# Attention and a squared-ReLU feed-forward on one core: the small products of the attention joined into fewer runs, and a second buffer for the weight ring of the last block

## The chip, the core and the metric

The kernel runs on one core of a Trainium2 chip. Its engines each take their instructions in order: TensorE (PE in the profile; its weight loads are PEld), VectorE (DVE), ScalarE (ACT), GpSimd (POOL) and SyncE (SP), which here issues nearly all DMAs. The metric is device time in microseconds of one execution; lower is better.

## The reference

Per batch (8) and head (8), with 576 rows of 64 numbers: a softmax of q over the row, a softmax of k over the sequence, then two products. The result, 4608 rows of 512, goes through a feed-forward with a squared ReLU.

```python
q_s = exp(q - max(q, -1));  q_s = q_s / (sum(q_s, -1) + 1e-9)
k_s = exp(k - max(k, 2));   k_s = k_s / (sum(k_s, 2) + 1e-9)
kv = einsum('bhsd,bhse->bhde', k_s, v)
x  = einsum('bhsd,bhde->bhse', q_s, kv)      # -> x: 4608 x 512
h  = maximum(x @ w_in, 0)                    # w_in: 512 x 2048
out = (h * h) @ w_out                        # w_out: 2048 x 512
```

## The kernel before

Everything is float32. The products of the feed-forward split each operand in a high and a low part of type fp32r and add three products; in the profile each is a matmul on the full 128*128 array with 512 or 256 columns. The products of the attention (k^T v, called kv, and q kv, called x) have contractions or outputs of 64 and use parts of the array: kv runs in shape 128*64, x in shape 64*64, and as plain float32 each of their matmuls is two records in the trace.

The 4608 rows are eight tiles t of 512 rows (the first 512 rows of each batch) and one tile of the eight tails of 64 rows. While the feed-forward of tile t runs, the attention of batch t+1 is made between its matmuls. Stages, in order of time:

- Tile 0 (to about 132 us), with the attention of batches 0 and 1 and the conversion of the weights from raw words (ACT scales, DVE and POOL join and split them). Until the first data are there PE runs filler transposes (`idle`).
- Tiles 1 and 2 (to about 309 us): per slice f of the hidden dimension `h` (12 matmuls) and `acc` (12 matmuls).
- Tiles 3 to 6 (to about 665 us) by Strassen's scheme on blocks, with half-width products `h<-w,ring` and `h<-w,w`. Sums of weight blocks lie in DRAM (`w_sums`) and come through a ring of buffers.
- The joint block (to about 750 us): tile 7 and the tails together, eight steps n of seven products (`pair_p1` to `pair_p7`, 6 matmuls of 512 columns each), with the ring loaded anew in each step, and the results kept in DRAM (`keep`, `g_b<-c`).
- The last product (`out`, L2015), and the writing of the result.

Up to the joint block the program records its operations, and a planner (class `Planner`) orders them with estimated durations: `order` takes, of what could start next, what has the longest path behind it (`tail`), shifted by lists of random seeds (`SEEDS` for tile 0, `LATER` for the rest). `place` and `possible` pick and grant PSUM banks: the small products share two banks (`choices`), which the joining of weight words uses too. `due` and `mark` tie an operation to a point in the chain of full matmuls. The joint block and the last product are written in program order.

Small products, from batch 2 on: `kv_product` makes kv of two pairs of heads (p-1, p) into two banks, each pair one unit of the plan (10 matmuls of 65 columns; column 65 is the sum of k). `kv_of` scales them on ACT. `x_products` then makes x of both pairs into the same banks: in turn 0 the 64 tail columns and the first 320, in turn 1 the last 192; ACT and DVE copy them out after each turn. Each matmul of x is a unit of its own, so that the planner may place them apart.

The ring: `load_ring(n, first)` loads the blocks of step n, in four groups: `a11` (768 KB, with `a12` and `s2`), `s1` and `s3` (256 KB each) and `a22` (512 KB, with `s4`). For `a11` there are two buffers (n even, n odd). `s1`, `s3` and `a22` have one each, so the load of step n+1 is issued behind the product of step n that read it. SP issues loads and stores in program order, and waits where a store's data aren't ready yet.

Of the kernel before, what the change touches and what calls it, by code (L numbers as in the profile page):

```python
# [132 lines left out]
class Planner:  # L133
# [92 lines left out]

    def place(self, b):
# [58 lines left out]
    def order(self):  # L286
# [12 lines left out]
        while ready:  # L299
            able = []  # L300
            for n in ready:
                t = max(free.get(n.engine, 0.0), n.since)
                if self.locked and n.port:
                    t = max(t, port)
                if n.behind is not None:
                    if n.behind.start is None:
                        continue
                    t = max(t, n.behind.start + n.behind.busy)
                for b in n.buffers:
                    if b.placed is not None:  # L310
                        continue
                    at, _ = self.place(b)
# [62 lines left out]
def attention_ffn(  # L375
# [29 lines left out]
    P = 128  # L405
# [25 lines left out]
    LATER = (  # L431
# [5 lines left out]
    )  # L437
# [11 lines left out]
    DUE = 3  # L449
    BURST = 450  # L450
    ON_ACT = 0
# [509 lines left out]
    def kv_product(b, *pairs):  # L961
# [3 lines left out]
        n = D if b == 0 else D + 1  # L965
        for p, ps in zip(pairs, two):
            with plan.together():
                kr, vr = made.pop(("ek", b, p)), made.pop(("v", b, p))
# [9 lines left out]
                for k_part, c in parts:  # L978
                    for j in range(2):
                        rows = slice((j ^ turn) * D, (j ^ turn) * D + D)  # L980
                        cols = slice(j * (D + 1), j * (D + 1) + n)
                        if b == 0:
                            of = vr[:, j, c, :] if c < C else v_heads[tl, 2 * p + j, 0:D].only(p // 2)
                        else:
                            of = vr[:, c, cols] if c < C else v_tail[:, p * W + cols.start:p * W + cols.stop]
                        T.matmul(
                            out=ps[rows, 0:n], lhsT=k_part[:, j * D:(j + 1) * D], rhs=of,
                            start=(c == 0), stop=(c == C), n=2 * n + BURST * (c == j == 0 and b > 1),
                        )

    def kv_scale(b, *pairs):
# [9 lines left out]
    def kv_of(b, *pairs):  # L1001

        kv_product(b, *pairs)
        kv_scale(b, *pairs)
        for p, ps in zip(pairs, made["kvp", b]):
            kv = small([P, D], "kvs", f"kv_{b}_{p}")
            S.activation(out=kv, in_=ps[:, 0:D], func=AF.Copy, scale=made.pop(("ks", p)), n=100)
            made["kv", b, p] = kv

    def x_product(b, p, x):  # L1010
# [26 lines left out]
        if p == NP - 1:  # L1037
            Y.dma_start(out=x_tail[:, :, b * TL:(b + 1) * TL], in_=made.pop(("xt", b)), kb=128)

    def x_products(b, p, x, turn):  # L1040

        pair = p - 1, p
        kvs, qts = [made["kv", b, i] for i in pair], [made["qT", b, i] for i in pair]
        two = made["kvp", b]
        FIRST = M - SPLIT

        def burst(begin, end, at):

            for j in range(2):
                for i in range(2):  # L1050
# [3 lines left out]
                        rhs=qts[i][rows, begin:end], start=True, stop=True,  # L1054
                        n=end - begin - 16 + BURST * (i == j == 0),
                    )

        def out_of(begin, end, at):

            n = end - begin  # L1060
            for i, (eng, one) in enumerate(((S.copy, two[0]), (V.tensor_copy, two[1]))):
                touched = [(pair[i] // 2, h) for h in range(begin // HM, 2)]
                eng(
# [4 lines left out]
        if turn == 0:  # L1068
            burst(M, SQ, SPLIT - TL)
            burst(0, FIRST, SPLIT)  # L1070
            if p == 1:
                made["xt", b] = small([P, NP, TL], "xt", f"xt_{b}", 1)
            xt = made["xt", b]
            S.copy(out=xt[:, pair[0], :].only(pair[0]), in_=two[0][:, SPLIT - TL:SPLIT], n=TL)
            V.tensor_copy(out=xt[:, p, :].only(p), in_=two[1][:, SPLIT - TL:SPLIT], n=TL)
            if b == B - 1:
                to = slabs[X_RAW + p // 2].bitcast(F32)[:, :, b * TL:(b + 1) * TL]
                Y.dma_start(out=to, in_=xt[:, pair[0]:p + 1, :], kb=64)
            elif p == NP - 1:
                Y.dma_start(out=x_tail[:, :, b * TL:(b + 1) * TL], in_=xt, kb=128)  # L1080
            out_of(0, FIRST, SPLIT)
        else:
            burst(FIRST, M, 0)
            out_of(FIRST, M, 0)
            for key in ("kv", "qT"):
                for i in pair:
                    made.pop((key, b, i))
            made.pop(("kvp", b))

# [620 lines left out]
    def strassen_pair(t, n, x_next, acc):  # L1710

        if n % 2 == 0:
            made["AB"] = [ps_h.tile([P, M], F32, tag="h", name=f"h_{t}_{n}_{i}") for i in range(2)]
# [11 lines left out]

        def two_units(slot):
            plan.due = now + 2
# [4 lines left out]
            plan.due = now + 2  # L1732
            unit(1)
            plan.due = None
# [34 lines left out]
        S.activation(out=c1[:, HM:M].only(1), in_=c1[:, HM:M].only(1), func=AF.Relu, n=HM)  # L1769
        two_units(slot_b)  # L1770
        block_product(t, n, A, "a22", "t4", False)
# [4 lines left out]
        V.tensor_tensor(out=gl1, in0=c1, in1=gh1, op=ALU.subtract)  # L1776
        block_product(t, n, Bk, "s4", "b22", False)
        ring_load(t, n + 1, "a22")
        plus(c0[:, HM:M].only(1), u2)
# [309 lines left out]
    for n in range(PAIRS):  # L2089
        if n == 0:  # L2090
            split_x_of("t4")
            unit(3)
        z = pair_begin(n)
        pair_p1(z)
        if n + 1 < PAIRS:
            load_ring(n + 1, "a11")
        if n == PAIRS - 1:
# [7 lines left out]
        if old:  # L2105
            pair_p4(old)
            pair_p3(old)
            load_ring(n, "a22")
        if n == PAIRS - 1:
# [7 lines left out]
        pair_p5(z)  # L2117
        if n + 1 < PAIRS:
            load_ring(n + 1, "s1")
        else:  # L2120
            for i in range(4):
# [7 lines left out]
        pair_p7(z)  # L2129
        if n + 1 < PAIRS:  # L2130
            load_ring(n + 1, "s3")
        if n == PAIRS - 3:
# [107 lines left out]
```

## Time and profile before

| | |
|---|---|
| median of 3 runs | 832.23 us (832.22 to 834.82) |
| profiled execution, its own time | 832.21 us |
| its span in the trace | 830.4 us |
| PE busy | 807.0 us, 97% (5085 matmuls) |
| PEld, DVE, ACT, POOL busy | 83%, 71%, 59%, 15% |
| DMA moved | 180.59 MB, mean 217 GB/s |
| chain that ended last | PE 84%, DMA 9%, ACT 2%, SP's queue 2%, DVE 1% |

The profiled execution took the time of the median, so times of its trace can be set against the median directly; 1.8 us lie outside its span. The busy time of PE counts matmuls whose latency overlaps that of the next. So the distance from one matmul's start to the next one's is what tells the cost, not the mean duration of one.

### The profile page before, as it was taken

Reading aid. Unit: us, or ns where it says so; the run is one execution under the profiler, and the core shown is the slowest. Engines: PE = TensorE matmul, PEld = TensorE weight load, DVE = VectorE, ACT = ScalarE, POOL = GpSimd, SP = SyncE. Lnnn points to the kernel's source line nnn. Section 1 sums busy time; section 2 is a strip of 40 time slices with the busy share of each in tenths; the row PEclk is TensorE's granted clock in tenths of the full one; section 3 lists DMA queues with packets and bytes.
Section 4 is the critical chain, followed back from the end, with each engine's and each line's share of the span. In section 5 each row is a group of like instructions: output and inputs, shape, how many; then the busy total and the mean of one; then the engine's idle time right before and its main releaser. Section 6 shows DMA issues by size and latency. Waiting matters only on the chain.

```text
span 830.4 us, 14550 instructions
## 1 busy us (share of the span) xinstructions
PE 807.0 (97%) x5085; PEld 691.3 (83%) x5085; DVE 589.0 (71%) x1206; ACT 489.5 (59%) x943; POOL 126.4 (15%) x145
## 2 busy tenths in 40 slices
PE   7989999999999999999999999999999998889997
PEld 6678878888787889898998989898888887778886
DVE  6888977785687657777678777777776732237995
ACT  5888855454465456656666576566665645456452
POOL 4899881100000000000000000000000000000000
PEclk9999999999999999999999999999999999999999
DMA  9993126776435368977988878889977459989666
GB/s 273 387 344 106 39 55 178 238 216 194 110 97 150 93 156 257 270 218 203 271 265 236 262 238 260 236 240 258 273 227 216 135 196 329 319 289 375 194 194 100
DMA packets 217353, 180.59 MB, mean 217 GB/s; under 512 B 133184, under 2 KB 184896, under 8 KB 217280
## 3 DMA queue, kind: packets, MB, share of 16 engines
q1 hardware_dynamic: 211360, 177.96, 71.1%
q10 hardware_dynamic: 5920, 1.71, 0.9%
q8 instruction: 40, 0.66, 0.3%
q14 instruction: 33, 0.27, 0.1%
HBM read 135.66 MB, written 43.38 MB: 216 GB/s over the span
## 4 chain that ended last, share of the span: by engine, by line
PE 84%; DMA 9%; ACT 2%; SPq 2%; DVE 1%; issue 1%; ACTq 0%; DVEq 0%
PE acc L101 34%; PE h L101 31%; PE out L2015 9%; PE kv L101 5%; PE h L1288 4%; DMA ring<-w_sums 3%; SPq L101 2%; DMA raw<-in_moe_w_out_dram 1%; DMA w<-w_sums 1%; DMA raw<-in_moe_w_in_dram 1%; ACT c L101 1%; DMA k<-in_k_dram 1%; DMA q<-in_q_dram 1%; DMA bst<-bst 1%; PE x L101 1%
## 5 line engine op out<-in xcount | busy, mean ns | idle before, releaser
L101 PE MATMUL acc<-w,gh 128*128 128x512 f32 x888 | 268.7, 384 | 2.3 <-DVE g L101 1.8
L101 PEld LDWEIGHTS acc<-w,gh 128*128 128x128 f32 x888 | 156.0, 190 | 26.9 <-issue 7.5
L101 PE MATMUL acc<-w,gl 128*128 128x512 f32 x444 | 168.4, 379 | 1.1 <-DVE gl L101 1.1
L101 PE MATMUL h<-x,w 128*128 128x512 f32 x576 | 135.4, 383 | 1.1 <-DVE x L101 0.6
L101 PEld LDWEIGHTS h<-w,ring 128*128 128x128 f32 x960 | 122.1, 191 | 8.3 <-issue 1.8
L101 PE MATMUL h<-w,ring 128*128 128x256 f32 x960 | 124.4, 276 | 0.0
L101 PEld LDWEIGHTS h<-x,w 128*128 128x128 f32 x576 | 107.1, 189 | 20.1 <-issue 2.9
L101 DVE TENSOR_TENSOR c<-h,u 128x256 f32<-128x256 f32 (+1 forms) x120 | 56.6, 475 | 94.0 <-ACT u L101 33.3
L101 ACT ACTIVATE c<-c 128x512 f32<-128x512 f32 (+1 forms) x166 | 97.8, 589 | 19.0 <-DVE c L101 16.2
L101 ACT COPY u<-h 128x256 f32<-128x256 f32 (+1 forms) x120 | 49.8, 415 | 98.0 <-PE h L101 74.0
L101 PEld LDWEIGHTS acc<-w,gl 128*128 128x128 f32 x444 | 83.9, 189 | 13.4 <-DVE gl L101 1.6
L101 POOL PARTITION_ALL_REDUCE kmx<-km x24 | 20.5, 853 | 477.2 <-DVE km L101 445.2
L2015 PE MATMUL out<-w,w 128*128 128x512 f32 x322 | 72.1, 379 | 0.0
L2015 PEld LDWEIGHTS out<-w,w 128*128 128x128 f32 x322 | 60.9, 189 | 8.6
L1288 PE MATMUL h<-w,ring 128*128 128x512 f32 x240 | 55.9, 387 | 8.0 <-DMA ring<-w_sums 8.0
L1288 PEld LDWEIGHTS h<-w,ring 128*128 128x128 f32 x240 | 45.5, 192 | 16.4 <-issue 8.1
L101 DVE TENSOR_TENSOR gl<-c,gh 128x512 fp32r<-128x512 f32 x64 | 44.1, 689 | 11.7 <-ACT gh L101 11.2
L101 ACT ACTIVATE gh<-r 128x512 fp32r<-128x512 f32 x47 | 29.7, 631 | 38.2 <-PE acc L101 38.0
L101 PEld LDWEIGHTS h<-w,w 128*128 128x128 f32 x384 | 47.8, 191 | 4.6 <-ACT c L101 1.1
L101 PE MATMUL h<-w,w 128*128 128x256 f32 x384 | 49.8, 277 | 0.3 <-DMA w<-w_sums 0.2
L101 ACT ACTIVATE r<-h 128x512 f32<-128x512 f32 x48 | 28.6, 595 | 35.2 <-PE h L101 33.2
L101 POOL TENSOR_TENSOR w<-w,w 128x512 fp32r<-128x512 f32 x32 | 41.2, 1297 | 4.3 <-ACT w L101 4.1
(176 smaller groups left out, 1123.3 us busy)
## 6 DMA issues: line engine op xcount, KB each, us to landing
ring<-w_sums SPq DMA_DIRECT2D x40, 768.0 KB, 5.6
w<-w_sums SPq DMA_DIRECT2D x40, 512.0 KB, 4.8
ring<-w_sums SPq DMA_DIRECT2D x80, 256.0 KB, 4.8
k<-in_k_dram SPq DMA_DIRECT2D x32, 256.0 KB, 4.4
raw<-in_moe_w_in_dram SPq DMA_DIRECT2D x16, 512.0 KB, 8.4
raw<-in_moe_w_out_dram SPq DMA_DIRECT2D x16, 512.0 KB, 9.2
w_sums<-w SPq DMA_DIRECT2D x32, 256.0 KB, 2.8
w<-wo_sums SPq DMA_DIRECT2D x32, 256.0 KB, 4.2
```

The source lines that it names most:

```text
L101: getattr(self.eng, op)(*map(real, args), **{k: real(a) for k, a in kwargs.items()})
L1288: nc.tensor.matmul(out=out.real(), lhsT=a[:, k * P:(k + 1) * P].real(), rhs=in_turn(m[k]).real(), start=(begin and k == 0 and i == 0), sto ...
L2015: nc.tensor.matmul(out=banks[name][m].real(), lhsT=a[:, m * P:(m + 1) * P].real(), rhs=in_turn(b[:, i, :]).real(), start=fresh and j == i ...
```

## The change

Three parts, and what the planner makes of them.

- **Joined runs.** `kv_product` becomes one unit: kv of both pairs, and behind it the tail columns of the x before (of the two pairs, or the batch, before), written into the same two banks at columns 128 to 191 (`tail_burst`, `tail_out`). The main 512 columns of x are one unit, `burst(0, M, 0)`, of four matmuls. For that the tail of q is transposed on its own into a tile `qtail` (48 DVE transposes in place of 24), and some tiles take other tags. Only the very last x (batch 7, last pairs) keeps two parts, 320 columns with the tail and 192. The estimate `BURST` of what a run costs is raised from 450 to 720 columns.
- **Second buffers in the joint block.** A new tile `ring_more` (in the place of `x_next`, which is free by then) takes `s1` and `s3` of steps 1, 3 and 5, and `slabs[6]` takes `a22` of these steps. So `s1`, `s3` and `a22` of step n+1 are issued a step earlier. Steps 6 and 7 keep the old order in part.
- **Planner and rest.** `possible` grants a bank in more cases, `place` gives two buffers of one unit two different banks, `LATER` is another list, `SEEDS` is the same. In the Strassen tiles the two PSUM tiles `AB` are taken once, and the load of `a22` and two units have other due points.

```diff
     def place(self, b, skip=0):
...
-            return min(
+            return sorted(
                 ((self.banks.get(c[1], 0.0), c) for c in b.choices), key=lambda x: x[0]
-            )
+            )[skip]
...
             known[n] = all(
-                o is b or o.placed is not None
+                o is b or o.placed is not None or o.choices and o.users[0] is b.users[0]
                 or (spare if len(o.choices) > 1 else self.place(o)[0] is not None)
+                or not o.choices and all(
+                    self.possible(u, b, known, spare)
+                    for u in (o.before.users if o.before else []) + (o.last.users[:1] if o.last else [])
+                )
                 for o in n.buffers
...
-    BURST = 450
+    BURST = 720
+    TAIL_AT = SPLIT - TL
...
-        V.transpose(out=qt, in_=t, n=590)
+        V.transpose(out=qt[:, 0:M], in_=t[:, 0:M], n=526)
...
+        V.transpose(out=made["qtail", b, p // 2][:, p % 2, :].only(p % 2), in_=t[:, M:SQ], n=TL)
...
-        for p, ps in zip(pairs, two):
-            with plan.together():
+        tails = made.pop("tails", None) if b >= TB else None
+        with plan.together():
+            for p, ps in zip(pairs, two):
...
+            if tails:
+                tail_burst(two, TAIL_AT, *tails)
+        if tails:
+            tail_out(two, TAIL_AT, *tails)
...
         if turn == 0:
-            burst(M, SQ, SPLIT - TL)
-            burst(0, FIRST, SPLIT)
...
+            with plan.together():
+                if alone:
+                    burst(0, FIRST, SPLIT)
+                    tail_burst(two, TAIL_AT, *tails)
+                else:
+                    burst(0, M, 0)
...
-    def load_ring(n, first):
+    def load_ring(n, first, joint=0):
...
-            to = slabs[7].rearrange("p t (i c) -> p (t i) c", c=HM)
+            to = slabs[6 if joint and n in (1, 3, 5) else 7].rearrange("p t (i c) -> p (t i) c", c=HM)
+        elif joint and n in (1, 3, 5) and first != "a11":
+            at = 2 * (first == "s3")
+            to = ring["more"][:, at:at + count, :].only(at)
...
+        z = pair_begin(n)
+        if n + 1 < PAIRS:
+            load_ring(n + 1, "a11", 1)
...
         pair_p1(z)
-        if n + 1 < PAIRS:
-            load_ring(n + 1, "a11")
+        if n + 2 < PAIRS:
+            load_ring(n + 1, "s1", 1)
+            load_ring(n + 1, "s3", 1)
+        if n == 0:
+            load_ring(1, "a22", 1)
```

On PE, batch 3, pairs 2 and 3, before: `kv_2`, `kv_3` are first the banks of kv (in `<-v,ek`) and then of x (in `<-qT,kv`).

```order
L101 MATMUL kv_2_2378<-v_2_1996,ek_2_2039 64x65 x8
L101 MATMUL kv_2_2378<-v_tail,kt_1526 64x65 x2
L101 MATMUL h_14_2392<-x_1_1603,w_1392 128x512 x3
L101 MATMUL kv_3_2405<-v_3_2022,ek_3_2222 64x65 x8
L101 MATMUL kv_3_2405<-v_tail,kt_1526 64x65 x2
L101 MATMUL kv_2_2378<-qT_2_2268,kv_2_2402 64x64 x2
L101 MATMUL kv_2_2378<-qT_2_2268,kv_2_2402 64x320 x2
L101 MATMUL h_14_2392<-x_1_1603,w_1392 128x512 x3
L101 MATMUL h_14_2392<-x_1_1618,w_1392 128x512 x3
L101 MATMUL kv_2_2378<-qT_2_2268,kv_2_2402 64x192 x2
```

The same pairs in the changed kernel, kv with the tails of pairs 0 and 1, and, 40 rows later, x:

```order
L101 MATMUL kv_2_2292<-v_2_2092,ek_2_2090 64x65 x8
L101 MATMUL kv_2_2292<-v_tail,kt_1564 64x65 x2
L101 MATMUL kv_3_2303<-v_3_2112,ek_3_2224 64x65 x8
L101 MATMUL kv_3_2303<-v_tail,kt_1564 64x65 x2
L101 MATMUL kv_2_2292<-qtail_0_1828,kv_0_2101 64x64
L101 MATMUL kv_3_2303<-qtail_0_1828,kv_1_2108 64x64
L101 MATMUL kv_2_2292<-qtail_0_1828,kv_0_2101 64x64
L101 MATMUL kv_3_2303<-qtail_0_1828,kv_1_2108 64x64
```

```order
L101 MATMUL acc_3_1748<-w_1467,gl_13_2472 128x512
L101 MATMUL kv_2_2292<-qT_2_2245,kv_2_2367 64x512
L101 MATMUL kv_3_2303<-qT_3_2464,kv_3_2370 64x512
L101 MATMUL kv_2_2292<-qT_2_2245,kv_2_2367 64x512
L101 MATMUL kv_3_2303<-qT_3_2464,kv_3_2370 64x512
L101 MATMUL acc_0_1726<-w_1552,gh_14_2485 128x512 x2
```

What were three rows of kv and x among full matmuls, and another for the second pair, are two runs; from batch 2 on there are 56 runs of small matmuls before and 25 in the changed kernel.

On SP, in the joint block, around the load of `a11` of step 3 (128x1536), before; `w<-wo_sums` are loads for the last product:

```order
L101 DMA g_b_0_7936<-c_0_7923 128x512
L101 DMA ring_3391<-w_sums_1855 128x512
L101 DMA g_b_0_7882<-c_1_7953 128x512
L101 DMA ring_3416<-w_sums_1855 128x512
L101 DMA w_586<-wo_sums_3886 128x2x256
L101 DMA w_710<-wo_sums_4314 128x2x256
L101 DMA ring_3416<-w_sums_1898 128x1536
```

And in the changed kernel:

```order
L101 DMA g_b_0_7883<-c_0_7870 128x512
L101 DMA g_b_0_7828<-c_1_7899 128x512
L101 DMA w_589<-wo_sums_3911 128x2x256
L101 DMA w_722<-wo_sums_4158 128x2x256
L101 DMA ring_3417<-w_sums_1901 128x1536
L101 DMA ring_more<-w_sums_1901 128x512 x2
```

The two loads of 256 KB (128x512), `s1` and `s3`, have moved from ahead of the 768 KB to behind it and belong to the next step; the store that stands ahead of the 768 KB is the same.

On PE in tile 0, at the attention of batch 1, before; the two halves `x_0_0` and `x_0_1` stand apart, 18 rows between them:

```order
L101 MATMUL acc_3_741<-w_842,gl_4_895 128x512
L101 MATMUL h_7_968<-x_0_400,w_917 128x512 x3
L101 MATMUL x_0_0_974<-qT_0_839,kv_0_914 64x288 x2
L101 MATMUL h_7_968<-x_0_400,w_917 128x512 x3
L101 MATMUL h_7_968<-x_0_524,w_917 128x512 x6
```

In the changed kernel they follow each other, three matmuls behind their kv:

```order
L101 MATMUL kv_0_941<-v_0_487,ek_0_853 64x65 x8
L101 MATMUL kv_0_941<-v_tail,kt_543 64x65 x2
L101 MATMUL acc_3_745<-w_864,gh_4_881 128x512 x2
L101 MATMUL acc_3_745<-w_864,gl_4_895 128x512
L101 MATMUL x_0_0_971<-qT_0_860,kv_0_965 64x288 x2
L101 MATMUL x_0_1_985<-qT_0_860,kv_0_965 64x288 x2
```

So tile 0 is ordered anew too, by the planner alone; the second half now stands where only the copy of the first half out of its bank, on ACT, separates them. At the start of the Strassen tiles the changed kernel has 18 full matmuls of `h` and `acc` between the last reader of the ring's first buffer and the first product that reads the ring.

## Rows read from the trace of the kernel before

**Rows 1.** Waits of PE, whole run: time in total, times, longest.

```profile
PE h L1288 <- DMA ring<-w_sums: 8.0, 5, 2.5
```

**Rows 2.** Busy time by stretch; after the stretch its length, then engines, PEclk, DMA share, GB/s.

```profile
500.00:550.00 50.00, 50.00 (x379) 44.05 (x378) 37.33 (x84) 28.88 (x66) 1.56 (x2) 1.00 0.87 251
```

**Rows 3.** Chain that ended last, in order of time: start, length, what.

```profile
198.26 2.59 PE h L101 x12
```

**Rows 4.** Timeline of PE, tile 2: start, length, instructions, count (kv and x: two records each).

```profile
203.37 0.69 PE L101 MATMUL kv<-v,ek 128*64 128x65 f32 x16
...
204.11 0.92 PE L101 MATMUL h<-x,w 128*128 128x512 f32 x3
204.95 0.69 PE L101 MATMUL kv<-v,ek 128*64 128x65 f32 x16
...
205.68 0.87 PE L101 MATMUL kv<-qT,kv 64*64 64x64 f32 x8
206.49 1.56 PE L101 MATMUL h<-x,w 128*128 128x512 f32 x6
207.98 0.54 PE L101 MATMUL kv<-qT,kv 64*64 64x192 f32 x4
208.45 0.92 PE L101 MATMUL h<-x,w 128*128 128x512 f32 x3
209.20 0.59 PE L101 MATMUL acc<-w,gh 128*128 128x512 f32 x2
209.63 0.38 PE L101 MATMUL acc<-w,gl 128*128 128x512 f32 x1
209.94 0.87 PE L101 MATMUL kv<-qT,kv 64*64 64x64 f32 x8
210.75 0.70 PE L101 MATMUL acc<-w,gh 128*128 128x512 f32 x2
```

**Rows 5.** Timeline of PE, tile 1: the first part of x of both pairs.

```profile
173.19 0.89 PE L101 MATMUL kv<-qT,kv 64*64 64x64 f32 x16
```

**Rows 6.** Instructions of the tile kv: the tails of k^T v, four records a pair.

```profile
L101 PE MATMUL kv<-v_tail,kt x112: 222/222/222, 62.8 to 639.3; 128*64 128x65 f32 x112
```

**Rows 7.** SP's timeline in the joint block, step 2.

```profile
688.11 0.38 SPq L101 DMA_DIRECT2D ring<-w_sums  x1
688.54 0.96 SPq L101 DMA_DIRECT2D w<-wo_sums  x2
689.55 0.47 SPq L101 DMA_DIRECT2D ring<-w_sums  x1
```

**Rows 8.** DMA issues, 665 to 750 us: count, KB each, median us to landing.

```profile
ring<-w_sums SPq DMA_DIRECT2D x6, 768.0 KB, 7.1
```

**Rows 9.** Timeline of PE in the joint block; in brackets the idle time before.

```profile
718.49 4.10 PE L1288 MATMUL h<-w,ring 128*128 128x512 f32 x12 [2.51 <-DMA ring<-w_sums]
```

**Rows 10.** Busy time by stretch, joint block and start of the last product (columns as Rows 2).

```profile
665.00:680.00 15.00, 15.00 (x71) 13.15 (x70) 5.92 (x10) 6.13 (x12) 1.41 (x1) 1.00 0.44 166
680.00:725.00 45.00, 39.49 (x172) 32.85 (x171) 11.60 (x17) 21.87 (x38) 0.00 (x0) 0.96 0.96 318
720.00:725.00 5.00, 5.00 (x17) 4.04 (x16) 1.39 (x2) 1.21 (x3) 0.00 (x0) 0.67 0.97 313
750.20:765.00 14.80, 14.80 (x70) 12.95 (x70) 11.35 (x14) 9.84 (x16) 0.00 (x0) 1.00 1.01 402
```

**Rows 11.** Busy time by stretch, tile 0 (columns as Rows 2).

```profile
60.00:80.00 20.00, 20.00 (x113) 16.06 (x113) 16.30 (x31) 16.36 (x24) 19.44 (x17) 1.00 0.45 154
```

**Rows 12.** ACT's instructions, 40 to 130 us: busy, mean ns; idle before.

```profile
L101 ACT CAST w<-w 128x1024 fp32r<-128x1024 f32 x14 | 14.6, 1040 | 1.4 <-POOL w L101 1.4
L101 ACT ACTIVATE gh<-r 128x512 fp32r<-128x512 f32 x15 | 9.5, 633 | 5.2 <-PE acc L101 5.1
L101 ACT COPY x<-x 128x288 f32<-128x288 f32 x4 | 1.6, 395 | 0.6 <-PE x L101 0.6
```

**Rows 13.** DMA issues, 303.5 to 305.5 us, the ring's first load (columns as Rows 8).

```profile
ring<-w_sums SPq DMA_DIRECT2D x1, 768.0 KB, 4.8
```

More of the change, by code (lines that the diff above doesn't have):

```diff
@@ L225, in add, with place @@
             b.seen.append((node, written, view.touched))
-    def place(self, b):
+    def place(self, b, skip=0):
         if b.choices:
@@ L308, in order @@
                     t = max(t, n.behind.start + n.behind.busy)
+                skip = 0
                 for b in n.buffers:
@@ L311, in order @@
                         continue
-                    at, _ = self.place(b)
+                    at, _ = self.place(b, skip if len(b.choices) > 1 else 0)
+                    skip += len(b.choices) > 1
                     if at is None:
@@ L765, in blocks_turn @@
         qt = att.tile([P, SQ], F32, tag=("qh", "ql")[p % 2], name=f"qT_{b}_{p}", bufs=1)
-        V.transpose(out=qt, in_=t, n=590)
+        V.transpose(out=qt[:, 0:M], in_=t[:, 0:M], n=526)
+        if p % 2 == 0:
+            made["qtail", b, p // 2] = att.tile(
+                [P, 2, TL], F32, tag="ekt", name=f"qtail_{b}_{p}", bufs=2
+            )
+        V.transpose(out=made["qtail", b, p // 2][:, p % 2, :].only(p % 2), in_=t[:, M:SQ], n=TL)
         made["qT", b, p] = qt
@@ L987, in kv_product @@
                             out=ps[rows, 0:n], lhsT=k_part[:, j * D:(j + 1) * D], rhs=of,
-                            start=(c == 0), stop=(c == C), n=2 * n + BURST * (c == j == 0 and b > 1),
-                        )
+                            start=(c == 0), stop=(c == C),
+                            n=2 * n if b < TB else 108 + BURST * (c == j == 0 and p == pairs[0]),
+                        )
+            if tails:
+                tail_burst(two, TAIL_AT, *tails)
+        if tails:
+            tail_out(two, TAIL_AT, *tails)
     def kv_scale(b, *pairs):
@@ L1005, in kv_of @@
         for p, ps in zip(pairs, made["kvp", b]):
-            kv = small([P, D], "kvs", f"kv_{b}_{p}")
+            kv = small([P, D], "dg" if b >= TB and p > 1 else "kvs", f"kv_{b}_{p}")
             S.activation(out=kv, in_=ps[:, 0:D], func=AF.Copy, scale=made.pop(("ks", p)), n=100)
@@ L1038, in x_product, with tail_burst, tail_out @@
             Y.dma_start(out=x_tail[:, :, b * TL:(b + 1) * TL], in_=made.pop(("xt", b)), kb=128)
+    def tail_burst(two, at, b, p, kvs, qtail):
+        for j in range(2):
+            for i in range(2):
+                rows, to = slice((j ^ i) * D, (j ^ i) * D + D), slice(j * D, (j + 1) * D)
+                T.matmul(
+                    out=two[i][to, at:at + TL], lhsT=kvs[i][rows], rhs=qtail[rows, i, :],
+                    start=True, stop=True, n=TL - 16,
+                )
+    def tail_out(two, at, b, p, kvs, qtail):
+        if p == 1:
+            made["xt", b] = small([P, NP, TL], "xt", f"xt_{b}", 1)
+        xt = made["xt", b]
+        S.copy(out=xt[:, p - 1, :].only(p - 1), in_=two[0][:, at:at + TL], n=TL)
+        V.tensor_copy(out=xt[:, p, :].only(p), in_=two[1][:, at:at + TL], n=TL)
+        if b == B - 1:
+            to = slabs[X_RAW + p // 2].bitcast(F32)[:, :, b * TL:(b + 1) * TL]
+            Y.dma_start(out=to, in_=xt[:, p - 1:p + 1, :], kb=64)
+        elif p == NP - 1:
+            Y.dma_start(out=x_tail[:, :, b * TL:(b + 1) * TL], in_=xt, kb=128)
     def x_products(b, p, x, turn):
@@ L1044, in x_products @@
         two = made["kvp", b]
+        tails = b, p, kvs, made["qtail", b, p // 2]
+        alone = (b, p) == (B - 1, NP - 1)
         FIRST = M - SPLIT
@@ L1054, in burst @@
                         rhs=qts[i][rows, begin:end], start=True, stop=True,
-                        n=end - begin - 16 + BURST * (i == j == 0),
+                        n=end - begin + 56 + BURST * (i == j == 0),
                     )
@@ L1061, in out_of @@
             for i, (eng, one) in enumerate(((S.copy, two[0]), (V.tensor_copy, two[1]))):
-                touched = [(pair[i] // 2, h) for h in range(begin // HM, 2)]
+                touched = [(pair[i] // 2, h) for h in range(begin // HM, 1 + (end - 1) // HM)]
                 eng(
@@ L1068, in x_products @@
         if turn == 0:
-            burst(M, SQ, SPLIT - TL)
-            burst(0, FIRST, SPLIT)
[L1071 to L1081, printed above, removed]
-        else:
-            burst(FIRST, M, 0)
-            out_of(FIRST, M, 0)
+            with plan.together():
[4 more added lines that the diff above has]
+                    burst(0, M, 0)
+            if alone:
+                tail_out(two, TAIL_AT, *tails)
+                out_of(0, FIRST, SPLIT)
+            else:
+                out_of(0, M, 0)
+        else:
+            if alone:
+                with plan.together():
+                    burst(FIRST, M, 0)
+                out_of(FIRST, M, 0)
+            else:
+                made["tails"] = tails
             for key in ("kv", "qT"):
@@ L1087, in x_products @@
                     made.pop((key, b, i))
+            made.pop(("qtail", b, p // 2))
             made.pop(("kvp", b))
@@ L1710, in strassen_pair @@
     def strassen_pair(t, n, x_next, acc):
-        if n % 2 == 0:
+        if "AB" not in made:
             made["AB"] = [ps_h.tile([P, M], F32, tag="h", name=f"h_{t}_{n}_{i}") for i in range(2)]
@@ L1724, in plus, with two_units @@
             V.tensor_tensor(out=as_rows(out), in0=in_rows(Bk), in1=as_rows(u), op=ALU.add, n=HM)
-        def two_units(slot):
-            plan.due = now + 2
+        def two_units(slot, due=2):
+            plan.due = now + due
             unit(1)
@@ L1731, in two_units @@
                 step_between(b, s, x_next)
-            plan.due = now + 2
+            plan.due = now + due
             unit(1)
@@ L1769, in strassen_pair @@
         S.activation(out=c1[:, HM:M].only(1), in_=c1[:, HM:M].only(1), func=AF.Relu, n=HM)
-        two_units(slot_b)
+        two_units(slot_b, 2 if n else 1.5)
         block_product(t, n, A, "a22", "t4", False)
@@ L1777, in strassen_pair @@
         block_product(t, n, Bk, "s4", "b22", False)
+        plan.mark(now + 1.5)
         ring_load(t, n + 1, "a22")
@@ L2091, in attention_ffn @@
             split_x_of("t4")
+            more = att.tile([P, NP, 2, HM], F32R, tag="x_next", name="ring_more")
+            ring["more"] = more.rearrange("p s t c -> p (s t) c")
+        z = pair_begin(n)
+        if n + 1 < PAIRS:
+            load_ring(n + 1, "a11", 1)
+        if n == 0:
             unit(3)
-        z = pair_begin(n)
         pair_p1(z)
-        if n + 1 < PAIRS:
-            load_ring(n + 1, "a11")
+        if n + 2 < PAIRS:
+            load_ring(n + 1, "s1", 1)
+            load_ring(n + 1, "s3", 1)
+        if n == 0:
+            load_ring(1, "a22", 1)
         if n == PAIRS - 1:
@@ L2107, in attention_ffn @@
             pair_p3(old)
-            load_ring(n, "a22")
+            m = min(n + 1, PAIRS - 1)
+            if n != PAIRS - 2:
+                load_ring(m, "a22", 1)
+            if n == m:
+                z.w.update((name, ring[name, n % 2]) for name in GROUPS["a22"])
         if n == PAIRS - 1:
@@ L2117, in attention_ffn @@
         pair_p5(z)
-        if n + 1 < PAIRS:
-            load_ring(n + 1, "s1")
-        else:
+        if n + 2 == PAIRS:
+            load_ring(n + 1, "s1", 1)
+        elif n == PAIRS - 1:
             for i in range(4):
@@ L2129, in attention_ffn @@
         pair_p7(z)
-        if n + 1 < PAIRS:
-            load_ring(n + 1, "s3")
+        if n + 2 == PAIRS:
+            load_ring(n + 1, "s3", 1)
         if n == PAIRS - 3:
```

10 rows, old and new, of the table LATER are left out of this document.

## The prediction

> **What bounds the kernel now.** I read the waits of PE first, then the busy time by stretch, then PE's timeline around the small products, and at last SP and the DMAs in the joint block. PE is the bound: from the middle of tile 0 to the joint block its columns are full, with DVE at about 37 and ACT at 29 of 50 us [rows 2]. Only one wait of PE is long in total, and it lies in the joint block: five waits for the ring, 8.0 us [rows 1]. So there are two things to gain: time that PE is "busy" with small products without streaming much, and these 8.0 us. Whatever stalls PE anew before 665 us counts in full.
>
> **What a run of small products costs.** Twelve full matmuls take 2.59 us, 0.216 each [rows 3]. From the first full matmul behind one run to the first behind the next, less 0.216 for each full matmul between, is what the next run costs [rows 4]:
> - 192 columns of x, one pair: 208.45 - 206.49 - 6 x 0.216 = 0.66 us.
> - 64 + 320 columns, one pair: 210.75 - 208.45 - 6 x 0.216 = 1.00 us.
> - kv of one pair: from its start at 203.37 to the next run's at 204.95, less 3 x 0.216, is 0.93 us.
> - kv with 64 + 320 columns of x right behind it: 206.49 - 204.11 - 3 x 0.216 = 1.73 us, 0.20 less than the two apart.
>
> Two pairs of x together take as long as one: 16 records last 0.89 us, 8 records 0.87 [rows 5, 4]. The slope is 0.34 us for 192 columns, so that 0.66 us for 192 is 0.34 of streaming and some 0.32 of getting in and out. This last is what joining saves.
>
> PE's timeline from batch 2 on has 56 runs. There are 24 kv (112 records of the tails of k^T v at four a pair are 28 pairs, less four of batch 1 [rows 6]); four of them have x right behind. I count 20 kv alone, 4 kv with x, 16 with 64 + 320 columns, 15 with 192, and one with a lone 64 (0.11 of streaming and 0.32, taken at 0.45): 18.6 + 6.9 + 16.0 + 9.9 + 0.5 = **51.9 us**.
>
> Of the new runs none is in the trace.
> - x of 512 columns, two pairs: 1.00 + 128 x 0.34 / 192 = 1.23 us. Eleven of them.
> - kv of two pairs: at most 1.86 - 0.20 = 1.66, as where shapes change. Between two parts of one shape a whole getting out and in of 0.32 should go: 1.86 - 0.32 = 1.54. I take 1.55.
> - The tails behind it: 64 x 0.34 / 192 = 0.11 of streaming, and the change of shape, 0.32 - 0.20 = 0.12 to 0.15: 0.25 us; at most a run of its own, 0.45. Eleven of them.
> - The last x keeps its two parts, 1.00 + 0.66.
>
> Sum: 11 x (1.55 + 0.25) + 1.55 + 11 x 1.23 + 1.66 = **36.5 us**, so 15.4 are saved; with the upper ends 11 x (1.66 + 0.45) + 1.66 + 13.5 + 1.7 = 40.1, 11.8 saved; below 0.25 nothing shows a tail for less than its streaming 0.11, so at most 17.
>
> A rule of the Trainium skill weighs on the tails: TensorEngine Tiling (Array Packing), Key Properties, says that changing the tiling mode, not just the tile, drains TensorE. By it kv and tails, of two shapes, save nothing by standing together, the 0.45 above, and 13 us would be saved in place of 15.4. The trace shows that kv and x of two shapes do save 0.20 when they stand together, so I keep 0.25.
>
> Beside this DVE gets 24 more transposes (64 columns) and loses 12 copies, as ACT does; with DVE busy 37 of 50 us [rows 2] I cost that at nothing. If DVE were late at one of them, PE would wait at the next run. A run now waits for the latest of both pairs' inputs; that is a rival below.
>
> **The joint block.** A step's seven products are 42 x 0.216 = 9.07 us. Every wait is for `a11` of the next step, 768 KB. SP issues it well into the step, since ahead of it in the queue stands the store of `c22`, made from the last product of the step before. In step 2 the issue is at 689.55, behind a load of 256 KB at 688.11 and two at 688.54 [rows 7]. The 768 KB take 7.1 us to land [rows 8], so PE is 1 to 2.5 us late. The change takes the 256 KB out of the way: its transfer at 318 GB/s [rows 10] is 0.8 us, its issue 0.4. The store of `c22` stays ahead. So five waits of 8.0 in sum lose 1.2 each, but those below 1.2 lose only what they have: I take **4.5 us** of gain, 3.5 stay. Behind one wait of 2.51 us the granted clock fell to 0.67 [rows 10], and 12 matmuls took 4.10 us in place of 2.59 [rows 9, 3]: 1.5 us, taken at 1.7 with those behind them. PE waited as long elsewhere at full clock; a shorter wait may spare it, and I take 1.0 of it. Together 5.5. The least is 1: in 680 to 725 us the DMAs were already 0.96 busy at 318 GB/s [rows 10], and a step moves 1.8 MB of ring, 1 MB of stores and 0.5 MB for the last product, 3.4 million bytes: at 318 / 0.96 = 331 GB/s that is 10.3 us a step, more than 9.07, and then every step stays late. The most is 10: 402 GB/s were moved in 750 to 765 us [rows 10], 8.5 us a step; and in 665 to 680 the DMAs stood at 0.44, which earlier loads can fill.
>
> The last product's loads also wait for stores and buffers that come earlier by what the block gains; its start is at 1.01 of DMA share already [rows 10]. PE waits for none of them now, and I take 0, at worst 2.
>
> **Tile 0.** The new order puts the second half of x of batch 1, pair 0, directly behind the first. There are two banks for small products, and the copy of the first half out of its bank stands on ACT behind a cast of weights and a square: 1.04 + 0.63 + 0.40 = 2.07 us from the scaling of kv [rows 12], less the first half's own 0.5: 1.6 us of PE's idle time where there was none [rows 11]. What else the new order does at the start can't be read from a row: POOL is busy 19.4 of 20 us there [rows 11], so that what it is given later stays late. I take another 1.4 us, with -1 and 4 as ends. Tile 0 loses **3 us** (0.5 to 6).
>
> **The start of the Strassen tiles.** The ring's first 768 KB can be issued when tile 2's last x is read; they take 4.8 us to land [rows 13]. In the new order 18 x 0.216 = 3.9 us of products remain to cover that (before, runs of x stood there too): **1 us** lost. At the turn of the tiles a run of kv no longer stands ahead of the first `acc`; I take **1 us** for four turns, 0 to 3.
>
> **Sum.** -15.4 - 5.5 + 3 + 1 + 1 = -15.9. Against 832.21, the profiled execution's own time, which is the median's, this is **816.3 us**.
>
> **Rivals.**
> 1. The joint block runs without waits and tile 0 loses little: -15.4 - 10 + 1.6 + 1 = -22.8, 809 us. For it: the DMAs reach 402 GB/s where loads stand in line. Against: the store ahead of `a11` stays. 0.17.
> 2. The joint block stays with the DMAs, at 10.3 us a step, and gains 1: 820.8 us. For it: 0.96 busy. Against: the windows at 402. 0.15. The Trainium skill, DMA: Bandwidth & Descriptors, Specifications, gives a core about 358 GB/s from HBM; by it a step would take 9.5 us, 0.5 late, an estimate near my 3.5 us of waits; 402 in these rows are above that limit.
> 3. Tile 0 loses 7 or more, since its order is a matter of POOL and its seeds were drawn for another order: 820 to 824 us. 0.15.
> 4. Slower: a joined run waits. It needs k, v, the sums and the banks of two pairs and the tail of a third, and PE, in order, stands still for the last. 24 runs; from 0.7 us of wait at each the 15.4 + 5.5 - 5 are used up, and with 0.9 it would be 837 us. Against it: 56 runs hardly waited before, and DVE and ACT have a quarter of their time free. 0.03.
> 5. The gains fail in part in several places, 830 to 834: 0.03.
>
> **How the numbers follow.** The forecast has 0.47, with 812 to 820 as its own bounds. From 808 to 825 I reach from the first rival to the third and leave some 2 in 10 out. This kernel's runs can be told apart by about 0.3%, 2.5 us: faster by more 0.94, within 0.03, slower 0.03.
>
> **What would show it.** In the changed trace, from the full matmul ahead of a joined kv to the one behind: 1.8 us more than the matmuls; x of 512: 1.2. PE's waits for the ring in the joint block: about 3.5 us in four or five, and PEclk without a slice below 1. In tile 0, a wait of PE of 1 to 2 us at x near 70 us for ACT, and a wait for the ring near 300. The forecast is wrong if joined runs wait for DVE or ACT, if the DMA share in 680 to 725 is 1.0 and the waits stay, or if tile 1 starts more than 6 us later than before.

## The result, and the profile after

The changed kernel takes **825.35 us** (median of 4 runs, 824.35 to 826.15), the kernel before 832.51: a ratio of 0.9907, 95% interval 0.9886 to 0.9929. It is faster by 7.2 us. The forecast was 15.9 us, 816.3, with a range of 808 to 825: the direction is right, the size is not, and the median lies just outside the range.

The profiled execution took 824.35 us, with a span of 822.6. First the waits of PE over the whole run (time in total, times, longest), which answer to [rows 1]:

```profile
PE h L1334 <- DMA ring<-w_sums: 7.3, 4, 2.2
PE acc L101 <- ACT gh L101: 2.2, 1, 2.2
PE x L101 <- ACT x L101: 1.0, 1, 1.0
PE h L101 <- DMA ring<-w_sums: 0.7, 1, 0.7
PE h L101 <- POOL w L101: 0.5, 1, 0.5
```

The joint block's waits, which the second buffers are there for, are nearly all still there: 7.3 us after 8.0. Four rows below them name places where PE had not waited before.

Next the small products, in PE's timeline (start, length, what, count). A joined kv without tails, one with tails, and an x of 512 columns; they answer to [rows 4]:

```profile
176.75 0.38 PE L101 MATMUL acc<-w,gl 128*128 128x512 f32 x1
177.06 0.69 PE L101 MATMUL kv<-v,ek 128*64 128x65 f32 x16
...
178.38 0.70 PE L101 MATMUL acc<-w,gh 128*128 128x512 f32 x2
178.91 0.38 PE L101 MATMUL acc<-w,gl 128*128 128x512 f32 x1
179.13 0.59 PE L101 MATMUL acc<-w,gh 128*128 128x512 f32 x2
...
197.18 0.81 PE L101 MATMUL h<-x,w 128*128 128x512 f32 x3
197.92 0.69 PE L101 MATMUL kv<-v,ek 128*64 128x65 f32 x16
...
199.24 0.34 PE L101 MATMUL kv<-qtail,kv 64*64 64x64 f32 x8
199.51 2.21 PE L101 MATMUL h<-x,w 128*128 128x512 f32 x9
201.56 0.59 PE L101 MATMUL acc<-w,gh 128*128 128x512 f32 x2
...
219.47 0.38 PE L101 MATMUL acc<-w,gl 128*128 128x512 f32 x1
219.78 1.09 PE L101 MATMUL kv<-qT,kv 64*64 64x512 f32 x8
220.80 0.70 PE L101 MATMUL acc<-w,gh 128*128 128x512 f32 x2
221.34 0.38 PE L101 MATMUL acc<-w,gl 128*128 128x512 f32 x1
221.55 0.59 PE L101 MATMUL acc<-w,gh 128*128 128x512 f32 x2
```

With 0.216 for each full matmul between, as in the prediction: kv of two pairs costs 179.13 - 176.75 - 4 x 0.216 = 1.52 us, with tails 201.56 - 197.18 - 12 x 0.216 = 1.79, x of 512 columns 221.55 - 219.47 - 4 x 0.216 = 1.22. None of the 25 runs waited: PE's idle time ahead of their matmuls is 0 in the trace.

**Where the 7.86 us between the two profiled executions lie** (832.21 to 824.35), from starts of matmuls in both traces. A run of small products is taken from the full matmul ahead of it to the sixth full one behind it, or the last ahead of the next run, less the full ones' own time:

| stretch | before | after | difference | forecast |
|---|---|---|---|---|
| tile 0, to the start of the 384th full matmul of `h` and `acc` | 132.17 | 137.25 | +5.1 | +3 |
| runs of small products behind it | 52.8 (56 runs) | 36.2 (25 runs) | -16.6 | -15.4 |
| first product of the Strassen tiles, late by | 0 | 0.9 | +0.9 | +1 |
| end of tile 6, last `acc`, late by | 1.5 | 4.5 | +3.0 | +1 (all tile turns) |
| smaller waits among full matmuls (what is left over) | | | +0.9 | 0 |
| start of the joint block to the last matmul | 159.1 | 157.1 | -2.0 | -5.5 |
| last matmul to the end (the last store) | 5.3 | 6.1 | +0.8 | 0 |
| sum | | | -7.9 | -15.9 |

So the joined runs did what they were forecast to do, and 1.2 us more. Against the forecast 3.5 us are missing in the joint block, 2.1 in tile 0, 2.0 at the end of tile 6, 0.9 in smaller waits and 0.8 in the last store.

At the end of tile 6 PE meets the 2.2 us of the second row above. Its wait there in the kernel before (in brackets the idle time), then its timeline now, and the busy time of 5 us around it (length, then PE, PEld, DVE, ACT, POOL, PEclk, DMA share, GB/s):

```profile
664.44 0.48 PE L101 MATMUL acc<-w,gl 128*128 128x512 f32 x1 [1.15 <-DVE gl L101]
```

```profile
655.33 0.70 PE L101 MATMUL acc<-w,gh 128*128 128x512 f32 x2 [2.21 <-ACT gh L101]
656.24 0.79 PE L101 MATMUL acc<-w,gl 128*128 128x512 f32 x1 [0.21 <-DVE gl L101]
656.83 1.06 PE L101 MATMUL acc<-w,gh 128*128 128x512 f32 x2
```

```profile
655.00:660.00 5.00, 4.46 (x12) 3.35 (x13) 4.20 (x7) 3.40 (x7) 1.51 (x1) 0.66 0.44 177
```

PE's order is the same as before there. ACT's is not: ahead of the cast that PE waits for (`gh`, at 654.66 us) now stand two casts for the joint block and the relu and square of the other slice. Behind the wait the clock falls to its lower level for a while (0.66 granted over these 5 us), and matmuls start up to 0.43 us apart in place of 0.216: the 20 behind the wait take 6.57 us, where run 1, with the same wait and no fall, takes 4.90.

In the joint block the waits look as before. SP's timeline in the step that PE began at 678.30 us, and PE's rows at its start and at the wait behind it; last, for comparison, the start of step 2 in the kernel before:

```profile
677.72 3.77 SPq L101 DMA_DIRECT2D g_b<-c  x2
681.53 0.98 SPq L101 DMA_DIRECT2D w<-wo_sums  x2
682.61 0.41 SPq L101 DMA_DIRECT2D ring<-w_sums  x1
683.12 0.91 SPq L101 DMA_DIRECT2D ring_more<-w_sums  x2
```

```profile
678.30 2.75 PE L1334 MATMUL h<-w,ring 128*128 128x512 f32 x12
...
689.41 2.83 PE L1334 MATMUL h<-w,ring 128*128 128x512 f32 x12 [1.88 <-DMA ring<-w_sums]
```

```profile
685.33 2.83 PE L1288 MATMUL h<-w,ring 128*128 128x512 f32 x12 [0.33 <-DMA ring<-w_sums]
```

The 256 KB load that stood ahead of `a11` in [rows 7] has gone behind it (`ring_more`), but the issue is still 4.3 us into the step (678.30 to 682.61), as it was in the kernel before (685.33 to 689.55 [rows 7]: 4.2). What holds SP is the second store of the first row, `c22`, whose data are ready only some 2.8 us into the step.

### The profile page after: what moved, and what is told of

It reads as the page before. It is cut to its first block, busy times and chain, and to the rows that moved or that the text cites. A ratio compares the mean times of both kernels' runs of the same rounds, so it can differ in the third digit from the quotient of the medians.

```text
span 822.6 us, 14396 instructions
## 1 busy us (share of the span) xinstructions
PE 791.9 (96%) x5000; PEld 685.7 (83%) x5000; DVE 588.1 (71%) x1219; ACT 489.1 (59%) x932; POOL 127.9 (16%) x145
## 4 chain that ended last, share of the span: by engine, by line
PE 82%; DMA 6%; DVE 3%; ACT 3%; POOL 1%; issue 1%; SPq 0%; POOLq 0%; DVEq 0%; ACTq 0%
PE acc L101 33%; PE h L101 31%; PE out L2065 9%; PE h L1334 5%; PE kv L101 4%; DMA ring<-w_sums 3%; DMA w<-w_sums 2%; ACT c L101 1%; DMA k<-in_k_dram 1%; DVE km L101 1%; DMA g_b<-c 1%; POOL w L101 1%; DVE w L101 0%; DVE up L101 0%; ACT gh L101 0%
## 5 line engine op out<-in xcount | busy, mean ns | idle before, releaser
L101 PEld LDWEIGHTS acc<-w,gh 128*128 128x128 f32 x888 | 157.1, 191 | 26.4 <-ACT gh L101 3.4
L101 PEld LDWEIGHTS h<-w,ring 128*128 128x128 f32 x960 | 121.7, 191 | 10.0 <-ACT gh L101 1.1
L101 DVE TENSOR_TENSOR c<-h,u 128x256 f32<-128x256 f32 (+1 forms) x120 | 57.0, 476 | 94.5 <-ACT u L101 36.5
L1334 PE MATMUL h<-w,ring 128*128 128x512 f32 x204 | 47.1, 381 | 7.3 <-DMA ring<-w_sums 7.3
L1334 PEld LDWEIGHTS h<-w,ring 128*128 128x128 f32 x204 | 38.4, 190 | 14.3 <-issue 8.8
L101 DVE TENSOR_REDUCE bst<-q 128x18 f32<-128x576 f32 x48 | 36.0, 749 | 17.0 <-DMA q<-in_q_dram 11.9
```

Source lines behind the costliest of these rows:

```text
L101: getattr(self.eng, op)(*map(real, args), **{k: real(a) for k, a in kwargs.items()})
L1334: nc.tensor.matmul(out=out.real(), lhsT=a[:, k * P:(k + 1) * P].real(), rhs=in_turn(m[k]).real(), start=(begin and k == 0 and i == 0), sto ...
```

## The experiments

Each ran beside the kernel before on the same chip, runs 1 to 4 on one chip and runs 5 to 8 on another. The median of the kernel before was 832.87 us on the first and 832.92 on the second, so medians of the two groups can be set side by side. "Less" is against the changed kernel's 825.35.

**Run 1: the old tile 0.** The rule that reorders tile 0 is taken out of the first plan.

```diff
-                o is b or o.placed is not None or o.choices and o.users[0] is b.users[0]
+                o is b or o.placed is not None
+                or self.locked and o.choices and o.users[0] is b.users[0]
...
-                or not o.choices and all(
+                or self.locked and not o.choices and all(
```

> The changed kernel with the planner's old rule for granting banks in its first plan only (tile 0). By the order of instructions tile 0 is then that of the kernel before, and everything behind it that of the changed kernel, on every engine. Theory: the new order of tile 0 costs 5.1 us (the 384th full matmul starts at 137.3 us, before at 132.2), and nothing gives them back: 820.3 us against 825.35, 384th full matmul at 132 to 132.5. Rival: later work was waiting anyway (the ring's first load, the end of the Strassen tiles), and the time is 823 to 825.

819.53 us (817.75 to 820.72): 5.8 less than the changed kernel. The 384th full matmul starts at 132.12. Nothing behind tile 0 absorbs what it loses. All ten profiles together tell the loss apart. From the 96th to the 384th full matmul the five with the old order take 74.74 to 74.78 us, the five with the new one 77.86 to 77.95: 3.1 us that belong to the order. The 96th itself starts at 57.3 to 58.6 us with the old order and at 57.4 to 59.5 with the new (four of the five at 59.3 or later): the rest, 0 to 2 us, is the start. It differs from execution to execution, but PE's order differs there too, from about 12 us on, so how much of it belongs to the order stays open.

Where the 3.1 us lie: 1.9 around small products, 1.3 in waits among full matmuls. PE's timeline of the changed kernel at the place that the prediction named:

```profile
72.08 0.70 PE L101 MATMUL x<-qT,kv 64*64 64x288 f32 x4
73.83 0.70 PE L101 MATMUL x<-qT,kv 64*64 64x288 f32 x4 [1.05 <-ACT x L101]
...
105.18 2.43 PE L101 MATMUL h<-x,w 128*128 128x512 f32 x10 [0.48 <-POOL w L101]
```

The two halves of x stand together, and the second waits 1.05 us for ACT's copy of the first.

**Run 2: the old joint block.** The loop of the joint block is that of the kernel before.

```diff
         z = pair_begin(n)
+        pair_p1(z)
         if n + 1 < PAIRS:
-            load_ring(n + 1, "a11", 1)
...
-        pair_p1(z)
-        if n + 2 < PAIRS:
-            load_ring(n + 1, "s1", 1)
-            load_ring(n + 1, "s3", 1)
...
+            load_ring(n + 1, "a11")
...
         pair_p5(z)
-        if n + 2 == PAIRS:
-            load_ring(n + 1, "s1", 1)
...
+        if n + 1 < PAIRS:
+            load_ring(n + 1, "s1")
...
```

> The changed kernel with the joint block's loop of the kernel before (one buffer each for s1, s3 and a22). Theory: the second buffers are worth the 2.0 us that the joint block and the last product took less from start to last matmul (159.1 before, 157.1 after): 827.3 us, waits of PE for the ring in the joint block near 8 us. Rival: most of these 2.0 us is a fall of the clock that was there before and not after, not the waits (8.0 and 7.3 us): then 825.5 to 826 us if the clock stays full here.

825.58 us (822.73 to 831.38, 12 runs): the time of the changed kernel. PE's waits in this joint block:

```profile
PE h L1334 <- DMA ring<-w_sums: 6.9, 5, 2.0
```

From the start of the block to the first product of the last stage it takes 82.2 us, and 82.2 in run 6 with the same block; with the second buffers the changed kernel takes 81.6, and runs 1, 4 and 8 take 79.7, 81.1 and 82.0. As they stand, the second buffers are worth between nothing and 2 us, which these runs can't tell apart.

**Run 3: `a11` ahead of the store.** One load is moved in program order, and so in SP's queue.

```diff
         z = pair_begin(n)
-        if n + 1 < PAIRS:
+        if n == 0:
             load_ring(n + 1, "a11", 1)
-        if n == 0:
             unit(3)
...
+        if n + 2 < PAIRS:
+            load_ring(n + 2, "a11", 1)
         pair_p7(z)
```

> The changed kernel with one move in the joint block: on SP the load of a11 (768 KB) of step n+2 stands ahead of the store of c22 of step n instead of behind it and behind two loads of the last product; same traffic, PE's order unchanged. Theory 1 (what stands ahead of a11 in SP's queue makes PE late): a11 is issued 3 to 4 us earlier, PE's waits for the ring fall from 7.3 us to below 2, 819 to 820 us. Theory 2 (the DMAs are full, some 3.4 million bytes a step at 331 GB/s are 10.3 us): something is late all the same, waits for the ring or w_sums stay above 5 us, 824 to 826 us.

816.22 us (814.27 to 818.92): 9.1 less, and so more than the 5 to 6 that theory 1 had. PE waits for no ring in the joint block any more: the chain of matmuls there is full, 9.07 us a step. SP's timeline, PE's, and the busy time of five steps and of one:

```profile
686.24 0.32 SPq L101 DMA_DIRECT2D g_b<-c  x1
687.08 0.32 SPq L101 DMA_DIRECT2D ring<-w_sums  x1
689.69 0.32 SPq L101 DMA_DIRECT2D g_b<-c  x1
```

```profile
692.01 1.46 PE L1334 MATMUL h<-w,ring 128*128 128x512 f32 x6
693.30 2.75 PE L1334 MATMUL h<-w,ring_more 128*128 128x512 f32 x12
695.89 2.75 PE L1334 MATMUL h<-w,ring 128*128 128x512 f32 x12
```

```profile
678.00:723.00 45.00, 45.00 (x210) 39.42 (x209) 13.82 (x20) 26.42 (x45) 0.00 (x0) 1.00 0.97 358
705.00:714.00 9.00, 9.00 (x43) 7.90 (x42) 2.76 (x4) 5.29 (x9) 0.00 (x0) 1.00 1.03 393
```

The 768 KB are issued at 687.08, ahead of the store at 689.69, and PE passes into the step that reads them (695.89) without a gap. The DMAs, whose share in [rows 10] was 0.96 at 318 GB/s, are at 0.97 with 358 and at 1.03 with 393. So theory 1 holds, and the DMAs were not full.

**Run 4: the last gh first.** The square, cast and difference of the last pair's `c1` get priority in the plan.

```diff
+        plan.ease = -9.0 * ((t, n) == (WT - 1, PAIRS - 1))
         S.activation(out=c1, in_=c1, func=AF.Square)
...
         V.tensor_tensor(out=gl1, in0=c1, in1=gh1, op=ALU.subtract)
+        plan.ease = 0.0
```

> The changed kernel with the cast of the last but one gh of tile 6 (gh_15) given priority on ACT, and its gl on DVE: it then stands right behind its square, ahead of two casts and the relu and square of the other slice. PE's order is unchanged. Theory: PE's wait of 2.2 us for it at 655 us goes, and with it the half clock of the nine matmuls behind it (some 2 us): 821.5 us, granted clock 1.00 throughout. Rival: gl_15 or the other slice is late in its place and the clock falls all the same: 824 to 825 us.

821.70 us (820.03 to 825.01), 3.7 less, where 3.8 was expected. That it came out so closely is in part luck: half of the sum was the half clock, which only three of six profiles show behind this wait (see the last section). PE's timeline there, without the wait and at the full clock:

```profile
653.35 0.38 PE L101 MATMUL acc<-w,gl 128*128 128x512 f32 x1
653.86 0.70 PE L101 MATMUL acc<-w,gh 128*128 128x512 f32 x2
654.58 0.48 PE L101 MATMUL acc<-w,gl 128*128 128x512 f32 x1
654.90 0.59 PE L101 MATMUL acc<-w,gh 128*128 128x512 f32 x2
```

The joint block starts at 656.2 in place of 659.4. "Granted clock 1.00 throughout" was wrong: behind a wait of 1.99 us for the ring at 686 us the clock fell here (0.66 granted over 686 to 691 us).

**Run 5: the three edits together.**

> The changed kernel with the three edits of the runs so far together: old rule for tile 0's plan, a11 ahead of the store of c22, gh_15 first on ACT. If the three are independent their gains add to the changed kernel's 825.35: 5.1 to 5.8 for tile 0, 9.1 for a11 (both by the medians of the runs), 3.2 for the end of tile 6 (start of the joint block 659.4 to 656.2): 807 to 809 us. Rival: PE, faster, meets another late DMA or ACT chain in the joint block or the last product: 811 to 814 us.

808.23 us (806.92 to 808.39), inside the 807 to 809 expected: together they take off 17.1 us, where the medians of the three add to 18.6. It is the best version, 0.9691 of the kernel before (0.9669 to 0.9714), and faster than the changed kernel by 17 us. Behind tile 0 this is all that PE waits for:

```profile
PE h L101 <- DMA ring<-w_sums: 0.7, 1, 0.7
...
PE acc L101 <- ACT o L101: 0.5, 3, 0.2
```

**Run 6: the joined runs alone**, the edits of runs 1 and 2 together.

> The changed kernel with the old rule for tile 0 and the old joint block, so the kernel before with the joined runs and their planning alone. Theory: the runs give 16.6 us, the ring's first load takes back 0.9, the end of tile 6 with its wait and half clock 1 to 3.5: 819 to 822 us, that is 832.2 - 12 and the same as with the new joint block (819.53), if that is worth nothing. Rival: the second buffers are worth 2 us: 821.5 or more.

820.10 us (816.9 to 821.7), beside 819.53 with the new joint block: the joined runs, with the planning that came with them behind tile 0, make the whole gain by themselves, 12.8 us against the kernel before, and more than the change as a whole. The planner's other changes (`LATER`, `AB`, the due points) were not taken apart from them.

**Run 7: the kernel before with `a11` early.** Run 3's move, with one buffer each for `s1`, `s3` and `a22`.

```diff
         pair_p1(z)
-        if n + 1 < PAIRS:
+        if n == 0:
             load_ring(n + 1, "a11")
...
+        if n + 2 < PAIRS:
+            load_ring(n + 2, "a11")
         pair_p7(z)
```

> The kernel before with one move: on SP the load of a11 of step n+2 ahead of the store of c22 of step n; one buffer each for s1, s3 and a22 as before. Theory: the store ahead of a11 was the whole cause of the waits, second buffers are not needed: PE's five waits (8.0 us) fall below 1 and the clock stays full, 822 us. Rival: with single buffers s1, s3 or a22 are late now, since they are issued behind the product of the step before: waits of 3 us or more stay, 825 to 828 us.

827.70 us (826.19 to 830.35): 5.2 less than the kernel before. My theory was wrong and the rival right. The waits move to other groups of the ring (the first row is for `a22`):

```profile
PE h L1288 <- DMA w<-w_sums: 3.5, 4, 1.8
PE h L1288 <- DMA ring<-w_sums: 2.2, 2, 1.3
```

So the early `a11` does a part alone, and needs the second buffers for the rest. From the block's start to the first product of the last stage: 84.2 us in the kernel before (with a fall of the clock; 82.2 in runs 2 and 6 with the same block and none), 79.3 with `a11` early, 81.6 with second buffers, 73.4 with both.

**Run 8: the changed kernel again.**

> The changed kernel again, beside the others on one chip: 825 us. Its half clock behind the wait of 2.2 us at 655 us: the old tile 0 and the old joint block had the same wait at the same place with full clock behind it (2.37 us to the next matmul each), so whether the clock falls may differ from run to run: then this profile has it or not, and the span goes with it by about 2 us (822.6 or 820.6).

825.69 us (821.51 to 827.75). The wait of 2.2 us at the end of tile 6 is there, at full clock this time; the clock fell in the joint block instead (see the last section).

## Why the prediction was right or wrong, step by step

- **The runs of small products: right.** 52.8 us before and 36.2 after were put at 51.9 and 36.5. (ACT is rid of 11 copies, not 12, since the last x keeps its two parts: 932 instructions after 943. Nothing hangs on it.) Kv of two pairs cost 1.52 (taken at 1.55), the tails behind it 1.79 - 1.52 = 0.27 (0.25), x 1.22 (1.23). Where the Trainium skill, TensorEngine Tiling (Array Packing), Key Properties, says that a change of mode drains TensorE, the prediction had put a tail by that rule at 0.45. At 0.27, of which 0.11 is streaming, the change of shape costs 0.16 where getting in and out of a run costs 0.32: a drain there may be, but it costs half of what standing alone does.
- **Joined runs don't wait: right.** PE stood still for none of them, with DVE busy 40 us and ACT 33 of 50.
- **The joint block: the term was mis-sized, from a wrong step.** This is the step of the prediction that failed, and the largest miss, 3.5 of 8.0 us. I gave each wait 1.2 us for the 256 KB load that moves from ahead of `a11`. Of this, 0.4 was its issue, and the store, now later in the step (2.8 us after 2.4), took that up; 0.8 was its transfer, which goes on beside `a11` all the same, since it now follows it in the queue (the 768 KB take 7.0 us to land, 7.1 before). I had seen the store ahead of `a11` and written that it stays, but did not make it the bound: it sets when `a11` can be issued, some 4 us behind the end of the step before, and moving the load ahead of it took the waits away (run 3). The block gained 2.0 in place of 5.5: 0.7 of waits for the ring in place of 4.5, and 1.7 because the clock fell in this block in the profile before and not in the one after, less 0.4 of a new wait for `w_sums`. That the clock did not fall is chance.
- **The second rival had the steps about right, for a reason that does not hold.** It took 0.96 busy at 318 GB/s as a limit, 10.3 us a step; the steps did take 9.1 to 11.5. Run 3 moved the same bytes in 9.07 us a step. Of the first rival, what spoke for it held (the DMAs can carry more, 393 GB/s over 9 us in run 3), and so did what spoke against it, the store ahead of `a11`, which decided. The third rival's time (820 to 824) lies nearest, but tile 0 lost 5.1, not 7 or more.
- **Tile 0: too small, and right in part by luck.** 3 us were forecast and 5.1 lost; taking the new order out gave 5.8 (run 1). Behind the 96th full matmul the order costs 3.1. Of that the wait for ACT's copy was 1.05 where I had 1.6; the other 1.4 had been taken without a row, so that the sum comes near 3.1 is luck. The rest lies ahead of the 96th, where executions differ by up to 2 us.
- **The start of the Strassen tiles: right**, 0.9 of 1. The first product of the ring started without a wait before, at 309.43 us; PE's timeline now:

```profile
310.66 1.58 PE L101 MATMUL h<-w,ring 128*128 128x256 f32 x12 [0.70 <-DMA ring<-w_sums]
```

- **The end of tile 6: not foreseen.** I had put 1 us for all four turns of the tiles, and this one lost 3.0. I looked for what ACT and DVE must do at the joined runs, not at what their new order does behind the last one. The wait is 1.1 us longer than before (2.2 after 1.1), and 1.7 us went to the half clock behind it in this profile, where the prediction had named full clock throughout as a sign. Run 4 shows the cause of the wait, a cast that stands too late on ACT.
- **The last store** landed 0.8 us later. It does not look like chance: from the start of the last matmul to the end it takes 5.7 to 6.1 us in all eight profiles with joined runs, and 5.3 and 5.0 in the two without (before, run 7). In SP's queue the last store stands behind stores of `x_joint`. SP is through with those 1.1 us after the last matmul began (817.58 and 816.51), 0.7 to 1.3 in all eight, and in the two without just as it began. Why they come later is open; no run was made on it.

## What to carry to other kernels

When a transfer is late, read first when it was issued and what stood ahead of it in its queue: a store whose data aren't ready holds every load behind it, and here neither buffers nor free bandwidth helped much until the load was moved ahead. A busy share of the DMAs near 1 is no proof that they are full; the bytes moved in the best stretch are the better measure. And where a planner orders the code, a rule that is loosened for one stage reorders the others too: compare the orders of all stages, and fence the rule in.

## What was not expected of the hardware

**The same wait may or may not bring the half clock.** These are 5 us around the same wait of 2.21 us for the same cast, with the same matmuls behind it, in the kernel with the old tile 0 (run 1), in run 8 and in run 6:

```profile
650.00:655.00 5.00, 3.95 (x17) 3.17 (x18) 4.70 (x8) 4.05 (x9) 1.00 (x1) 1.00 0.51 197
```

```profile
652.00:657.00 5.00, 3.98 (x17) 3.20 (x18) 4.67 (x8) 4.05 (x9) 1.03 (x1) 1.00 0.49 191
...
685.00:690.00 5.00, 4.34 (x12) 3.56 (x13) 0.00 (x0) 1.59 (x3) 0.00 (x0) 0.66 1.04 403
708.00:713.00 5.00, 4.89 (x23) 4.34 (x24) 1.38 (x2) 1.68 (x4) 0.00 (x0) 1.00 1.03 363
```

```profile
650.00:655.00 5.00, 4.20 (x10) 3.07 (x11) 4.46 (x8) 3.66 (x8) 1.25 (x1) 0.66 0.44 179
```

Of six profiles with this wait (after, and runs 1, 2, 3, 6 and 8) three have half the clock behind it and three the full one; in run 8 the clock fell instead behind a wait of 2.30 us for the ring, and not behind one of 2.39 us in the same block. Each of these falls cost 1.5 to 1.7 us (the 20 matmuls behind the wait at 655 us take 6.41 to 6.59 us with it, 4.90 without), and so did those in the joint block of the kernel before and of run 4 (1.7). So what a wait costs is its length and, by what looks like chance, some 1.6 us more; the profiles without a wait over 2 us behind tile 0 (runs 5 and 7) have no fall there. The six executions of run 8 agree: at a mean granted clock of 0.997 and 0.995 they took 821.51 and 824.85 us, at 0.990 to 0.992 between 825.33 and 827.75. The Trainium skill, TensorE: Matmul & The Clock Gate, Part 1, says of a kernel's start that the chip's look at activity runs free of the program, so that the same kernel can measure differently. The three and three, of a wait in mid-kernel, agree with that, but no run shows that this is their cause.

**The DMAs' busy share hardly moves with what they carry**: 0.96 at 318 GB/s before [rows 10], 0.97 at 358 and 1.03 at 393 in run 3, for the same loads and stores.
